# The transpose of the first weight matrix: from TensorE and ScalarE to crossbar transfers issued by SyncE

## The chip, the cores and the metric

The kernel runs on one core of one Trainium2 chip. A core has TensorE (PE, matrix products into PSUM), VectorE (DVE), ScalarE (ACT), GpSimd (POOL) and SyncE (SP, which here only issues transfers), and 16 DMA engines that move data between HBM and SBUF and inside SBUF. Each engine works through its own queue of instructions in order; semaphores hold an instruction until what it needs is there. The metric is device time in microseconds (us) for one execution; times given are medians of several runs.

## The reference

Inputs are x (8 x 4160 x 192), weight_gen (8 x 4160 x 8 heads x 7 taps), and three matrices w1, w2 (192 x 1024) and w_out (1024 x 192), all float32. First a dynamic convolution over time with softmax weights, then a two-layer network that takes the larger of two hidden products:

```python
w = softmax(weight_gen, axis=-1)                     # over the 7 taps
y[b, s, h, :] = sum_k w[b, s, h, k] * x_pad[b, s + k, h, :]
h1, h2 = y @ w1, y @ w2
out = np.maximum(h1, h2) @ w_out
```

x_pad is x with six rows of zeros ahead of each sequence. The output has 33280 rows of 192.

## The kernel before

**The split of the mathematics.** The maximum is written as max(h1, h2) = h1 + relu(h2 - h1). So the kernel computes a hidden product with the difference wd = w2 - w1, a relu on ACT, and a product with w_out (wo); and it adds y @ (w1 @ w_out). The 192 x 192 matrix w1 @ w_out is called w10. It is formed once, on TensorE, in w10_product (line 650): 16 matmuls whose stationary operand is w1t, the transpose of w1 with the 1024 hidden channels on the partitions, in eight blocks of 128 x 192, and whose moving operand is wo. w10_copies (line 662) then moves it from PSUM to the tile w10 (shown in the profile as "w") by three copies on ACT. How w1t comes about is what the change is about.

**Tiling.** The 33280 rows lie as 260 columns of 128 partitions. They go through in batches of 16 columns; a batch is loaded as xb_t (16 columns and a halo of 6 columns that is copied from the batch before, load_halo, line 123) and wg_t (the raw softmax weights). ACT takes exponentials (exp_sum, weights) and logarithms (ln), DVE sums (red) and subtracts (shift). DVE's mul (line 173) multiplies x by the weights for all 7 taps into m_t; adds (line 188) sums the taps into y_t. For the first two batches units of 4 columns are used instead: PE sums the taps and transposes them at once (sum_transpose, line 239) and ACT casts the result to yt. From the third batch on, transpose (line 212) has SP issue a crossbar transfer from y_t to yt, SBUF to SBUF.

**Products.** hid_tile (line 291) multiplies a tile of yt with wd into PSUM (hdp, later hd); relu moves it to rd_t; out_first (line 345) adds y @ w10 and the products of rd_t with wo, out_second the other half of the rows; evac (line 377) copies results to o_t, and SP stores them.

**Order.** The order on each engine is written out by hand (a manual schedule): what is emitted first runs first on its engine. The stretch of the change is the prologue, lines 512 to 693. SP issues the loads of the first weights and of the first x in order, the last being load_wg(1, ...) (line 553). POOL issues two further pieces of x for batch 0, w_out, the first half of x for batch 1 and its halo, in that order. ACT copies w1 in float32 (tiles ws) to bf16 in three pieces, as w1["E"] (rows 0 to 127 of w1, two halves of 512 channels, lines 578 and 633) and w1["T"] (rows 128 to 191, where partitions 0 to 63 hold channels 0 to 511 and partitions 64 to 127 the others, line 632). PE does a matmul on an identity matrix at the start (keep_warm), the first tap sums and the hidden tiles 0 to 3, then w1_transposed (line 594), hidden tiles 4 and 5, a tap sum, hidden tiles 6 and 7, and w10_product. The tile tp of w1_transposed takes a turn in a pool of two PSUM pairs (tag "op") that yps, pw and op_ps share. ACT copies tp to w1t after the relus of tiles 4 and 5 (line 673). behind(first, load) makes a load wait for another instruction.

Of the kernel before, what the change touches and what calls it, by code (L numbers as in the profile page):

```python
# [9 lines left out]
FP32 = mybir.dt.float32  # L10
BF16 = mybir.dt.bfloat16
# [12 lines left out]
def kernel(  # L24
# [9 lines left out]
    nc = tc.nc  # L34

    B, S, D = x.shape
    H, K = weight_gen.shape[2], weight_gen.shape[3]
    F = moe_w1.shape[1]
    P = 128
    PAD = K - 1  # L40
    WGC = H * K
    FCH = F // P
    HF = F // 2
# [20 lines left out]
    for b, (c0, n) in enumerate(BATCHES):  # L64
# [21 lines left out]
    ps = {k: first_ps.enter_context(tc.tile_pool(name="pps_" + k, bufs=2, space=bass.MemoryType.PSUM))  # L86
          for k in ("h", "o")}
# [22 lines left out]
    def load_x(b, o, n, halo=True):  # L110

        if b not in xb_ts:
            xb_ts[b] = pxb.tile([P, (16 + PAD) * D], BF16, name="xb_t", tag="xb")
        load = nc.gpsimd.dma_start(  # L114
            out=xb_ts[b][:, (PAD + o) * D:(PAD + o + n) * D],
            in_=bass.AP(tensor=x.tensor, offset=(BATCHES[b][0] + o) * D,
                        ap=[[CPP * D, P], [1, n * D]]),
        )
        if b > 0 and o == 0 and halo:
            load_halo(b)  # L120
        return load
# [37 lines left out]
    def weights(b, o):  # L159

        w = dict(pieces(b))[o]
        if b not in en_ts:
            en_ts[b] = pen.tile([P, 16 * WGC * 2], BF16, name="en_t", tag="en")
        J = 2 if w == 4 and b < 2 else 1
        N = w * H // J
        for j in range(J):
            nc.scalar.activation(  # L167
                out=_sub(en_ts[b], (o * WGC + j * N * K) * 2, [[2 * N, K], [2, N], [1, 2]]),
                in_=_sub(wg_ts[b], (o * H + j * N) * K, [[1, K], [K, N], [0, 2]]), func=AF.Exp,
            )  # L170


    def mul(b, o):

        n = dict(pieces(b))[o]
        if n == 4 and b < 2:
            m_out = _sub(m_t, K * o * D, [[64, 2], [P, K * 6], [1, 64]])
            x_in = _sub(xb_ts[b], o * D, [[2 * D, 2], [D, K], [1, 2 * D]])
        else:
            m_out = m_t[:, K * o * D:K * (o + n) * D]  # L180
            x_in = _sub(xb_ts[b], o * D, [[D, K], [1, n * D]])
        return nc.vector.tensor_tensor(  # L182
            out=m_out, in0=x_in,
            in1=_sub(en_ts[b], o * WGC * 2, [[2, K * n * H], [0, G // 2], [1, 2]]),
            op=ALU.mult,
        )
# [46 lines left out]
    def half(j):  # L233
        return slice(64 * j, 64 * j + 64)
# [56 lines left out]
    def hid_tile(t):  # L291


        u = TILES[t][0]
        fs, w = chunks(t)
        for f in fs:
            for s in range(3):
                for j in range(2):
                    nc.tensor.matmul(  # L299
                        hid_out(t, f, j), lhsT=wd_at(j, s, f // 4, f % 4 * P, P),  # L300
                        rhs=_sub(yt_ts[u][half(j), :], (s + j) % 3 * P, [[3 * P, w // P], [1, P]]),
                        start=(f == fs[0] and s == 0), stop=(f == fs[-1] and s == 2),
                        skip_group_check=True,
                    )
# [121 lines left out]
    OUTS, c = [[], [], []], 0  # L426
# [8 lines left out]
    def room(g):  # L435

        t0, n = GROUPS[g]
        if "c" in ps:
            ab = ps["ab"].tile([P, 2048], FP32, name="hd2", tag="ab")
            for t in range(t0, t0 + n - 1):  # L440
                hd_at[t] = ab, (t - t0) * 1024
            hd_at[t0 + n - 1] = ps["c"].tile([P, 1024], FP32, name="hd1", tag="c"), 0
        else:
            for t in range(t0, t0 + n):
                hd_at[t] = ps["h"].tile([P, 1024], FP32, name="hdp", tag="hd"), 0
        rd = prd.tile([P, 3 * 1024], BF16, name="rd_t", tag="rd")
        for t in range(t0, t0 + n):
            rd_at[t] = (rd, t - t0)
        return rd
# [56 lines left out]
    ident = consts.tile([P, P], BF16, name="ident")  # L506
# [5 lines left out]
    with tc.tile_pool(name="pstage", bufs=1) as pstage:  # L512
# [7 lines left out]
        for p0, p1 in ((1, 16), (16, P)):  # L520
            nc.sync.dma_start(  # L521
                out=xs[p0:p1, 0:PAD * D],
                in_=bass.AP(tensor=x.tensor, offset=(p0 * CPP - PAD) * D,
                            ap=[[CPP * D, p1 - p0], [1, PAD * D]]),
# [20 lines left out]
        for wi, wsrc in enumerate((moe_w1, moe_w2)):  # L545
            for h in range(2):
                nc.sync.dma_start(
                    out=ws["T", wi][half(h), :],
                    in_=bass.AP(tensor=wsrc.tensor, offset=P * F + h * HF, ap=[[F, 64], [1, HF]]),
# [20 lines left out]
        for o in (0, 4, 8, 12):  # L570
            weights(0, o)
        nc.vector.tensor_copy(out=xb_ts[0][:, PAD * D:(PAD + 4) * D],
                              in_=xs[:, PAD * D:(PAD + 4) * D])
        first_mul = mul(0, 0)
        w1 = {kind: pstage.tile([P, w], BF16, name="w1" + kind)
              for kind, w in (("E", F), ("T", HF))}
# [14 lines left out]

        w1t = pstage.tile([P, FCH * D], BF16, name="w1t")

        def w1_transposed():

            tp = ps["o"].tile([P, 1024], FP32, name="tp", tag="op")[:, :].bitcast(BF16)
            for at, kind, nr in ((0, "E", P), (P, "T", 64)):
                for fi in range(FCH):
                    o = fi // 4 * 1024 + fi % 4 * D
                    rows, c = (slice(0, P), fi) if kind == "E" else (half(fi // 4), fi % 4)  # L600
                    nc.tensor.matmul(
                        tp[:, o + at:o + at + nr],
                        lhsT=w1[kind][rows, c * P:(c + 1) * P],
                        rhs=ident[rows, rows], is_transpose=True, skip_group_check=True,
                    )
            return tp

        warm = ps["h"].tile([P, 1024], FP32, name="warm", tag="hd")

        def keep_warm(times):  # L610
# [11 lines left out]
            out=wo[:, :].rearrange("p (f d) -> p f d", d=D),  # L622
            in_=bass.AP(tensor=moe_w_out.tensor, offset=0, ap=[[D, P], [P * D, FCH], [1, D]]),
# [7 lines left out]

        nc.scalar.copy(out=w1["T"], in_=ws["T", 0])
        nc.scalar.copy(out=w1["E"][:, HF:F], in_=ws["E", 0][:, HF:F])
        rd = room(0)
        hid_tile(0)
        relu(rd, 0, 1)
# [8 lines left out]
        ln(1)  # L645
        shift(1)
        mul(0, 12)
        tp = w1_transposed()

        def w10_product():  # L650

            pw = ps["o"].tile([P, 1024], FP32, name="pw", tag="op")
            for at, c0 in ((0, 0), (512, 64)):
                for fi in range(FCH):
                    nc.tensor.matmul(
                        pw[:, at:at + D], lhsT=w1t[:, fi * D + c0:fi * D + c0 + P],
                        rhs=wo[:, fi * D:(fi + 1) * D],
                        start=(fi == 0), stop=(fi == FCH - 1), skip_group_check=True,
                    )
            return pw  # L660
# [9 lines left out]
        hidden(2)  # L670
        behind(relu_of[5], load_wg(2, nc.gpsimd))
        load_x(1, 8, 8)
        for h in range(2):
            nc.scalar.copy(out=w1t[:, 4 * h * D:4 * (h + 1) * D], in_=tp[:, h * 1024:h * 1024 + 4 * D])
        weights(1, 0)
        mul(1, 0)
        sum_transpose(2)
# [142 lines left out]
```

## Time and profile before

| | us |
|---|---|
| median of 3 runs (lowest to highest) | 411.19 (410.9 to 411.44) |
| profiled execution, from its first to its last instruction | 409.1 |
| PE busy | 398.8 |
| DVE busy | 374.4 |
| ACT busy | 357.4 |
| POOL busy | 68.7 |
| the transposes of w1 on PE (line 601), two groups of 8 | 0.62 and 0.30 |
| the copies tp to w1t on ACT (line 674), 2 | 1.56 |

The profile gives no other time of that execution than its span. It is one execution; "busy" counts neither waits nor the issue of transfers. A share of busy time is a mean over stages with different limits, so what a change in one stretch is worth has to be read there: from the timeline of that stretch, from the waits and from the chain of waits that ended last.

### The profile page before, as it was taken

The page shows a single profiled execution, that of the slowest core. Times are in us where ns is not written, and L with a number is a line of the kernel's source. Part 1 is how long each engine was busy: PE and PEld are TensorE (multiplying, and loading weights), DVE is VectorE, ACT ScalarE, POOL GpSimd, SP SyncE. Part 2 cuts the span into 40 slices and gives each one's busy share as a digit, 9 for nine tenths or more (in the row PEclk, how much of TensorE's full clock was granted, in tenths as well). Part 3 has the DMA queues.
Part 4 walks back from the last instruction along what each step waited for, and adds up shares of the span by engine and source line. Part 5 has one row for each costly group of instructions (what it writes and reads, how often), then busy time and mean ns, then how long its engine had stood idle before and what let it go on. Part 6 is the DMA issues. An engine that isn't in the chain of part 4 may idle for free.

```text
span 409.1 us, 15992 instructions
## 1 busy us (share of the span) xinstructions
PE 398.8 (97%) x7350; PEld 317.1 (78%) x7350; DVE 374.4 (92%) x219; ACT 357.4 (87%) x424; POOL 68.7 (17%) x101
## 2 busy tenths in 40 slices
PE   7999999999999999999999999999999999999995
PEld 2688999677777777777777777777787777787795
DVE  6999999999999999999999999999999999999000
ACT  6899989999999988999988999988999989888771
POOL 0321101222211021221101221210122212210000
PEclk9999999999999999999999999999999999999998
DMA  8966667658657874963796497489648648744513
GB/s 245 250 152 164 116 151 186 143 143 184 150 97 219 217 118 99 260 176 74 224 195 146 96 251 180 82 195 238 120 106 241 166 64 244 151 89 79 213 61 136
DMA packets 60384, 65.68 MB, mean 161 GB/s; under 512 B 47615, under 2 KB 48511, under 8 KB 60318
## 3 DMA queue, kind: packets, MB, share of 16 engines
q1 hardware_dynamic: 51934, 40.54, 36.0%
q0 software_dynamic: 8240, 24.04, 29.5%
q8 instruction: 57, 0.93, 0.9%
q10 hardware_dynamic: 144, 0.10, 0.1%
q14 instruction: 9, 0.07, 0.1%
HBM read 35.96 MB, written 25.56 MB: 150 GB/s over the span
## 4 chain that ended last, share of the span: by engine, by line
DVE 73%; PE 17%; issue 4%; DMA 4%; SPq 0%; DVEq 0%; ACT 0%
DVE m_t L182 37%; DVE m_t L198 15%; DVE m_t L204 10%; PE op_ps L339 9%; PE hd L299 7%; DVE sum_t L147 3%; DVE y_t L207 3%; DVE wg_t L156 3%; DMA xs<-in_x_dram 3%; PE op_ps L351 2%; DMA yt<-y_t 1%; DVE wd L582 0%; DVE xb_t L618 0%; SPq L521 0%; SPq L104 0%
## 5 line engine op out<-in xcount | busy, mean ns | idle before, releaser
L309 ACT ACTIVATE rd_t<-hd 128x1024 bf16<-128x1024 f32 (+1 forms) x206 | 234.6, 1189 | 28.0 <-PE hd L299 26.5
L339 PE MATMUL op_ps<-wo,rd_t 64*128 64x192 bf16 x4160 | 210.6, 243 | 0.1
L339 PEld LDWEIGHTS <-rd_t 64*128 64x128 bf16 x4160 | 180.8, 94 | 15.7 <-ACTq L372 0.3
L299 PE MATMUL hd<-yt,wd 64*128 64x512 bf16 (+1 forms) x1584 | 187.3, 360 | 1.4 <-ACT rd_t L309 1.2
L182 DVE TENSOR_TENSOR m_t<-xb_t,en_t 128x10752 bf16<-128x10752 bf16 (+1 forms) x37 | 187.4, 5071 | 0.2
L299 PEld LDWEIGHTS <-wd 64*128 64x128 bf16 x1776 | 94.1, 94 | 43.3 <-issue 3.3
L224 POOL CAST gate<-yt 128x1 f32<-128x1 bf16 x29 | 34.0, 1171 | 275.7 <-DMA yt<-y_t 275.7
L198 DVE TENSOR_TENSOR m_t<-m_t 128x4608 bf16<-128x4608 bf16 (+1 forms) x32 | 76.8, 2401 | 0.1
L395 ACT COPY o_t<-op_ps 128x384 f32<-128x384 f32 (+1 forms) x99 | 57.3, 591 | 13.4 <-PE op_ps L339 13.3
L351 PE MATMUL op_ps<-w,yt 64*128 64x192 bf16 x780 | 55.5, 243 | 1.1 <-ACT o_t L395 1.0
L351 PEld LDWEIGHTS <-yt 64*128 64x128 bf16 x780 | 38.4, 94 | 17.5 <-issue 2.1
L204 DVE TENSOR_TENSOR m_t<-m_t 128x3072 bf16<-128x3072 bf16 (+1 forms) x29 | 50.0, 1724 | 0.1
L167 ACT ACTIVATE en_t<-wg_t 128x896 bf16<-128x896 f32 (+2 forms) x45 | 35.3, 820 | 0.0
L207 DVE TENSOR_TENSOR y_t<-m_t 128x1536 bf16<-128x1536 bf16 (+1 forms) x29 | 27.3, 941 | 0.5
L385 DVE COPY o_last<-op_ps 128x192 f32<-128x192 f32 x1 | 0.4, 358 | 25.9 <-ACT o_last L385 25.9
L156 DVE TENSOR_TENSOR wg_t<-wg_t,sum_t 128x280 f32<-128x280 f32 (+5 forms) x46 | 22.0, 481 | 0.0
L147 DVE TENSOR_REDUCE sum_t<-e_t 128x64 f32<-128x448 f32 (+2 forms) x31 | 19.6, 636 | 2.6 <-ACT e_t L135 2.6
L114 POOL DMA_DIRECT2D xb_t<-in_x_dram x33 | 17.7, 535 | 23.3 <-ACT rd_t L309 11.8
L135 ACT ACTIVATE e_t<-wg_t 128x896 f32<-128x896 f32 (+2 forms) x18 | 16.1, 899 | 2.5 <-DMA wg_t<-in_weight_gen_dram 2.5
L309 ACT ACTIVATE rd_t<-hdp 128x1024 bf16<-128x1024 f32 x16 | 16.2, 1048 | 0.6 <-PE hdp L299 0.6
L613 PE MATMUL warm<-ident 128*128 128x512 bf16 x38 | 11.0, 457 | 2.6 <-DVE ident L560 2.6
L299 PE MATMUL hdp<-yt,wd 64*128 64x256 bf16 x192 | 12.9, 269 | 0.1
(46 smaller groups left out, 73.6 us busy)
## 6 DMA issues: line engine op xcount, KB each, us to landing
out_dram<-o_t SPq DMA_DIRECT2D x28, 768.0 KB, 5.0
xb_t<-in_x_dram POOLq DMA_DIRECT2D x30, 384.0 KB, 5.2
wg_t<-in_weight_gen_dram POOLq DMA_DIRECT2D x14, 448.0 KB, 5.2
xb_t<-xb_t POOLq DMA_DIRECT2D x16, 288.0 KB, 5.2
out_dram<-o_t SPq DMA_DIRECT2D x8, 384.0 KB, 2.9
wg_t<-in_weight_gen_dram SPq DMA_DIRECT2D x2, 448.0 KB, 4.5
xs<-in_x_dram SPq DMA_DIRECT2D x2, 384.0 KB, 6.0
xb_t<-in_x_dram POOLq DMA_DIRECT2D x3, 192.0 KB, 5.1
```

Source lines behind the costliest of these rows:

```text
L156: nc.vector.tensor_tensor(out=w_t, in0=w_t, in1=_sub(s_ts[b], hs.start, [[1, hs.stop - hs.start], [0, K]]), op=ALU.subtract)
L167: nc.scalar.activation(out=_sub(en_ts[b], (o * WGC + j * N * K) * 2, [[2 * N, K], [2, N], [1, 2]]), in_=_sub(wg_ts[b], (o * H + j * N) * K ...
L182: return nc.vector.tensor_tensor(out=m_out, in0=x_in, in1=_sub(en_ts[b], o * WGC * 2, [[2, K * n * H], [0, G // 2], [1, 2]]), op=ALU.mult,)
L198: nc.vector.tensor_tensor(out=taps(0, 1, 3), in0=taps(0, 1, 3), in1=taps(3, 1, 3), op=ALU.add)
L204: nc.vector.tensor_tensor(out=taps(0, 2, 2), in0=taps(0, 2, 2), in1=taps(1, 5, 2), op=ALU.add)
L207: nc.vector.tensor_tensor(out=_sub(y_ts[b], o * D, [[64, 2], [P, 3 * w // 2], [1, 64]]), in0=taps(0, 1, 1), in1=taps(2, 1, 1), op=ALU.add,)
L224: nc.gpsimd.tensor_copy(out=gate, in_=yt[:, 0:1])
L299: nc.tensor.matmul(hid_out(t, f, j), lhsT=wd_at(j, s, f // 4, f % 4 * P, P), rhs=_sub(yt_ts[u][half(j), :], (s + j) % 3 * P, [[3 * P, w // ...
L309: relu_of[t0] = nc.scalar.activation(out=rd[:, k * 1024:(k + n) * 1024], in_=hd[:, at:at + n * 1024], func=AF.Relu)
L339: return nc.tensor.matmul(op_out(c), lhsT=rd[half(r), k * 1024 + at:k * 1024 + at + P], rhs=wo[half(r), f * D:(f + 1) * D], start=False, s ...
L351: nc.tensor.matmul(op_out(c + j), lhsT=yt_ts[u][half(j), (3 * i + (s + j) % 3) * P:(3 * i + (s + j) % 3 + 1) * P], rhs=w10[half(j), s * D: ...
L395: nc.scalar.copy(out=_sub(o, c % 24 * D, [[D, len(qs)], [h * D, 2], [1, D]]), in_=_sub(tile_, at + (qs[0] - p) * D, [[D, len(qs)], [512, 2 ...
```

## The change

The 16 transposing matmuls and ACT's two copies from PSUM to w1t are taken out. In their place SP issues four crossbar transfers that read the bf16 copies of w1 in SBUF and write w1t in SBUF: one for each half of w1["E"] (128 partitions by 512) and one for each half of w1["T"] (64 partitions by 512). They are emitted directly after ACT's last copy of w1, in the order E first half, T first half, T second half, E second half. SP issued nothing between load_wg(1, ...) and the first output store before. w10_product and all that follows stay as they are.

```diff
         w1t = pstage.tile([P, FCH * D], BF16, name="w1t")
 
-        def w1_transposed():
-
-            tp = ps["o"].tile([P, 1024], FP32, name="tp", tag="op")[:, :].bitcast(BF16)
-            for at, kind, nr in ((0, "E", P), (P, "T", 64)):
-                for fi in range(FCH):
-                    o = fi // 4 * 1024 + fi % 4 * D
-                    rows, c = (slice(0, P), fi) if kind == "E" else (half(fi // 4), fi % 4)
-                    nc.tensor.matmul(
-                        tp[:, o + at:o + at + nr],
-                        lhsT=w1[kind][rows, c * P:(c + 1) * P],
-                        rhs=ident[rows, rows], is_transpose=True, skip_group_check=True,
-                    )
-            return tp
+        def w1_transposed(kind, h):
+
+            out_ = w1t[:, 4 * h * D:4 * (h + 1) * D].rearrange("p (f d) -> p f d", d=D)
+            if kind == "E":
+                nc.sync.dma_start_transpose(out=out_[:, :, 0:P], in_=w1["E"][:, h * HF:(h + 1) * HF])
+            else:
+                nc.sync.dma_start_transpose(out=out_[:, :, P:D], in_=w1["T"][half(h), :])
...
         nc.scalar.copy(out=w1["T"], in_=ws["T", 0])
         nc.scalar.copy(out=w1["E"][:, HF:F], in_=ws["E", 0][:, HF:F])
+        for kind, h in (("E", 0), ("T", 0), ("T", 1), ("E", 1)):
+            w1_transposed(kind, h)
...
         mul(0, 12)
-        tp = w1_transposed()
-
         def w10_product():
...
         load_x(1, 8, 8)
-        for h in range(2):
-            nc.scalar.copy(out=w1t[:, 4 * h * D:4 * (h + 1) * D], in_=tp[:, h * 1024:h * 1024 + 4 * D])
         weights(1, 0)
```

## The prediction

> **What bounds the kernel now.** I read the page first, section 1 for the busy shares:
>
> ```profile
> ## 1 busy us (share of the span) xinstructions
> PE 398.8 (97%) x7350; PEld 317.1 (78%) x7350; DVE 374.4 (92%) x219; ACT 357.4 (87%) x424; POOL 68.7 (17%) x101
> ```
>
> TensorE (PE) and VectorE (DVE) are both nearly full, so a saving on one of them counts only where the other does not hold it back. The chain of waits, in order of time (start, length, what), says who does, around the change and late in the kernel:
>
> ```profile
> 12.90 0.57 DVE xb_t L618
> ...
> 25.73 5.82 DVE m_t L182 x2
> ...
> 328.23 5.23 DMA yt<-y_t
> 333.50 0.82 PE hd L299 x6
> ```
>
> From 12.90 to 328 us the chain lies on DVE. The trace has only 0.76 us of idle DVE time between 12.7 and 328.3 us. At 328.23 a crossbar transfer carries the last such y_t to yt, PE picks it up at 333.50, and from there PE sets the end. The list of waits says how tight that meeting is (us in total, times, longest):
>
> ```profile
> PE hd L299 <- DMA yt<-y_t: 0.2, 1, 0.2
> ```
>
> PE waits for a crossbar transfer once in the whole kernel, 0.2 us, at 333.3. I set each unit's landing beside PE's first hidden-layer matmul on it: the margin is 7.3 us for the first transfer (issue 56.23), 2.6 us near 215 us and 0.04 us at 333.45. PE idles 3.8 us in all after 2.0 us, so it runs almost without a break and slowly catches up with DVE. Hence two paths end together. A DVE delay early on comes out at the end whole, less about 0.04 us; a PE delay comes out less what later waits absorb; a PE or ACT gain comes out only until PE meets DVE, some 0.2 us.
>
> Next the timeline of the stretch that is changed (start, length, engine, line):
>
> ```profile
> 19.41 0.62 PE L601 MATMUL tp<-ident,w1E 128*128 128x128 bf16 x8
> 19.96 0.30 PE L601 MATMUL tp<-ident,w1T 64*128 64x64 bf16 x8
> ...
> 22.00 1.02 PE L248 MATMUL yps<-ident,m_t 64*128 64x64 bf16 x57
> ...
> 22.98 1.56 ACT L674 COPY w1t<-tp 128x768 bf16<-128x768 bf16 x2
> ...
> 25.12 1.49 PE L655 MATMUL pw<-wo,w1t 128*128 128x192 bf16 x16
> ```
>
> **Part one, what goes away.** PE loses 16 transposes, 0.62 + 0.30 = 0.92 us. They lie between hidden tiles 3 and 4. Tile 4 needs the PSUM buffer that ACT's relu of tile 2 empties (19.16 plus about 1.02 = 20.18), and its first matmul starts at 20.26 already; tile 5 waits for the next relu, about 21.15. Then sum_transpose(2) starts at 22.00, as DVE finishes mul(0, 8) (19.00 + 2.95 = 21.95). So the 0.92 us turn into waits for ACT and DVE, and nothing moves at 22.00: 0 us. ACT loses two copies, 2 x 0.866, 1.56 us on the clock with their overlap. What follows in ACT's queue is weights(1, 0), then the cast of yps, which needs PE's sum_transpose(2) (23.32 + 0.56 = 23.88), relu 6, and w10_copies, which need PE's w10_product (25.12 + 1.49 = 26.61; the first copy starts at 26.65). PE reaches w10_product through sum_transpose(2) and hidden tiles 6 and 7 (23.71 + 1.48 = 25.19), none of which waited for the copies. So ACT idles before 26.65 and continues as before: 0 us. DVE's mul(1, 0) had its weights at 24.35 + 0.80 = 25.15 and starts at 25.73 because DVE is full; earlier weights bring nothing. Half of a PSUM pair comes free sooner (tp no longer has a turn), but pw and the next yps take buffers that were empty before too. If all of this cover failed, the most it could bring is 0.92 us of PE, since ACT's 1.56 us run beside it.
>
> **Part two, what is added: issue.** Four crossbar transfers on SP's queue, behind load_wg(1, ...) at 10.03; the next SP instruction is the first output store at 32.41, so SP is free in between and nobody stands behind them. The first waits for ACT's copy of w1E (10.01 + 0.60 = 10.61), the second and third for w1T (14.78 + 0.62 = 15.40), the fourth for the other half of w1E (15.30 + 0.62 = 15.92). The nearest rows are those of the yt transfers, in the list of DMA issues (median us from issue to landing) and in the rows on yt (ns for which SP is held: least, median, most):
>
> ```profile
> yt<-y_t SPq DMA_TRANSPOSE x29, 3.9
> ```
>
> ```profile
> L216 SPq DMA_TRANSPOSE yt<-y_t x29: 1316/1435/2807, 56.2 to 379.2; - x29
> ```
>
> With a hold of 1.4 us each, SP starts the second at 15.4, the third at 16.8, the fourth at 18.2. A whole yt (12 blocks, 1536 packets of 256 bytes) lands in 3.6 to 5.4 us; the fourth is a third of that, so 18.2 + 5.4 = 23.6 is late for it. PE needs the first half of w1t at 25.12 and the second half four matmuls later, about 25.5. Margin 1.9 us: 0 us on PE. With the longest hold each time (2.81) the fourth starts at 21.0 and lands by 26.4 at worst, 0.9 us too late. I take the median, as the chunks are smaller than a yt.
>
> The Trainium skill speaks against the change here: "VectorE: DVE Perf Modes", section "The three transpose paths", puts a 128x128 bf16 transpose at 390 ns on TensorE and 1309 ns through the DMA crossbar, and its rules take TensorE where PSUM will do as destination. By an estimate from that page, the twelve blocks' worth one after another would last 12 x 1.309 = 15.7 us from 15.4, and PE would stall about 6 us (near 417 us); the rows above, 12 blocks in 3.9 us, don't agree with such a sum.
>
> **Part three, what is added: traffic.** The four move 8 blocks of 128x128 and 8 of 64x128, again 1536 packets of 256 bytes if a half block costs half. Alone, a yt's packets pass in 2.0 us on all 16 engines; where PE's instruction fetch falls among them they take 3.0 to 3.5, and by the time that packets were held the dearest came to 4.1. The windows (length, PE, PEld, DVE, ACT, POOL, clock, DMA share, GB/s) show what they meet:
>
> ```profile
> 16.00:18.00 2.00, 1.83 (x96) 1.47 (x92) 1.92 (x6) 2.00 (x3) 0.00 (x0) 1.00 1.28 156
> 18.00:20.00 2.00, 1.99 (x34) 1.45 (x32) 2.00 (x2) 2.00 (x3) 0.54 (x1) 1.00 1.29 207
> 20.00:22.00 2.00, 1.92 (x33) 1.34 (x33) 2.00 (x2) 2.00 (x4) 0.00 (x0) 1.00 0.69 197
> 22.00:24.00 2.00, 1.70 (x91) 1.57 (x92) 2.00 (x2) 2.00 (x4) 0.56 (x2) 1.00 0.05 18
> ```
>
> The DMA engines are full with POOL's loads until about 21 us and then almost idle until POOL's next load (issue 23.44). The first transfer stands behind wg_t's load in SP's queue (landing 15.3) and meets xb_t columns 8 to 15: these land at 17.0 and 17.8, needed at 19.00 and 22.86, so 0.7 to 1.4 us there are covered. wo lands at 20.8, needed at 25.12: covered. Tight is mul(1, 0) at 25.73: its columns land at 22.6 and its halo (xb_t<-xb_t, issue 18.41) at 23.6, 2.1 us ahead. Delay between 0 (the transfers use gaps) and 4.1 us (dearest row, all of it added to the slowest engine); I take 2.0, the uncontended row, because those engines are idle after 22: landing 25.6, still 0.1 us early. Sum: 0 us.
>
> **Part four, phases.** PE has 32 fewer instructions (16 matmuls, 16 weight loads), at some 35 such instructions a us 0.9 us of its stream, so its instruction fetches shift against the yt transfers. One fetch at 331.3 to 332.2 stretched the transfer behind the 0.2 us wait; it may now miss it, or hit another whose margin is near 1 us. Worth -0.2 to +0.4 us; I take 0. Total: span 409.1 + 0 + 0 + 0. The median of the runs, 411.2, lies 2.1 us above the span (the profile gives no other time of that execution), and I carry that over: 411.2 us.
>
> **The rivals.** *Slower: the halo comes late.* The place is mul(1, 0) on DVE at 25.73; behind it in DVE's queue stand all later products, with 0.76 us of idle time in 316 us to make it up. It decides from a delay of 2.1 us on; a loss over 0.8 us needs 3.0. At 4.1 us the stall is 2.0 us: about 413.2 us. For it: no row shows a crossbar transfer beside sustained POOL loads, and a single 16 KB fetch on one engine already costs one 1.0 to 1.5 us. Against: idle engines from 22 us.
> *Slower: w1t comes late.* If each of the four waits until the one before has landed (the yt transfers are 6 to 12 us apart and can't show it), then at a yt's 3.9 us the last lands at 15.4 + 3 x 3.9 = 27.1, 1.6 us after 25.5. Behind w10_product stand w10_copies and weights(1, 4) on ACT (28.38, for DVE's mul(1, 4) at 28.60), so DVE stalls 1.4 us: 412.6 us. Against: the pieces are a third and a sixth of a yt.
> *Faster: the 0.92 us of PE come through*, if relu and DVE do not hold 20.2 and 22.0, and the fetch leaves 333 us: 411.2 - 0.92 = 410.3. Against: the margin of 0.04 us at 333.45 and DVE's full queue.
>
> **The numbers.** Measurement can tell about 0.2% (0.8 us) from no change. Covered everywhere 0.67, with small stalls under 0.8 us in it; halo late by more 0.14; w1t late by more 0.13; faster 0.06. Prediction 411.2; the range goes from 410.6 (runs spread 0.3 below the median, and the phases) to 413.0, which takes in most of both slow cases. Faster 0.06, within 0.2% 0.67, slower 0.27.
>
> **What would show it.** Right: no L601 and no w1t<-tp rows; four transfers landing before 25.1; PE's L655 at 25.1; DVE's products at 22.86 and 25.73 without idle time before them; ACT idle 0.7 us or so before L664; PE's wait for yt still near 333 us. Wrong: idle DVE time before L182 put down to xb_t<-xb_t or xb_t<-in_x_dram (halo), or PE waiting at L655 for w1t with the following DVE product late (w1t), or sum_transpose(2) before 22.0 (faster).

## The result, and the profile after

The changed kernel took 414.10 us (median of 10 runs, 413.55 to 416.27), the kernel before 411.27 beside it on the same chip (10 runs, 410.65 to 413.95): a ratio of 1.0066 with a 95% interval from 1.0044 to 1.0088. It is slower by 2.8 us, and lies 1.1 us above the upper end of the predicted range.

The profiled execution took 414.07 us with a span of 412.3 us, 3.2 us more than the span of before. Section 1 of its page, and from section 4 the shares of the chain that ended last:

```profile
PE 398.4 (97%) x7334; PEld 317.0 (77%) x7334; DVE 374.7 (91%) x219; ACT 356.4 (86%) x422; POOL 69.0 (17%) x101
...
PE 83%; ACT 10%; DMA 3%; issue 2%; DVE 0%; SPq 0%; DVEq 0%; ACTq 0%
```

PE lost its 32 instructions and ACT its two copies, and no engine became busier in a way that would explain 3.2 us. What grew is waiting. The chain now runs over PE to the end, where before it lay on DVE for 73% of the span; its stretch in the prologue says where the time went (start, length, what):

```profile
21.29 0.83 PE hdp L299 x12
22.13 1.20 PE yps L248 x73
23.33 2.47 issue
25.80 0.35 PE yps L248 x11
26.15 2.56 PE hdp L299 x24
28.71 1.79 PE pw L649 x16
30.52 0.48 ACT w L658
```

In the middle of sum_transpose(2) PE stands for 2.47 us, and the releaser is "issue": no semaphore, no other engine, no transfer of data. The 73 matmuls before and the 11 after belong to the same loop over the same tile. Before, a stop of 0.30 us stood in the same sum (23.02 to 23.32). In the timeline of the kernel before, with the wait before a group in brackets:

```profile
23.32 0.56 PE L248 MATMUL yps<-ident,m_t 64*128 64x64 bf16 x27 [0.30 <-issue]
23.71 1.48 PE L299 MATMUL hdp<-yt,wd 64*128 64x256 bf16 x24
```

The timeline of the changed kernel shows SP's issues, then PE, DVE and ACT:

```profile
10.92 1.32 SPq L598 DMA_TRANSPOSE w1t<-w1E  x1
15.54 2.46 SPq L600 DMA_TRANSPOSE w1t<-w1T  x2
18.10 1.23 SPq L598 DMA_TRANSPOSE w1t<-w1E  x1
...
25.80 0.35 PE L248 MATMUL yps<-ident,m_t 64*128 64x64 bf16 x11 [2.47 <-issue]
25.96 2.75 PE L299 MATMUL hdp<-yt,wd 64*128 64x256 bf16 x24
28.64 1.84 PE L649 MATMUL pw<-wo,w1t 128*128 128x192 bf16 x16
...
26.79 2.96 DVE L182 TENSOR_TENSOR m_t<-xb_t,en_t 128x5376 bf16<-128x5376 bf16 x1 [0.90 <-DMA xb_t<-xb_t]
32.28 2.96 DVE L182 TENSOR_TENSOR m_t<-xb_t,en_t 128x5376 bf16<-128x5376 bf16 x1 [2.53 <-ACT en_t L167]
...
30.52 0.48 ACT L658 CAST w<-pw 128x384 bf16<-128x384 f32 x1 [2.03 <-PE pw L649]
```

After the stop the hidden tiles 6 and 7 (line 299) last 2.75 us instead of 1.48, and w10_product 1.84 instead of 1.49. The windows say why (length, PE, PEld, DVE, ACT, POOL, clock, DMA share, GB/s):

```profile
22.00:24.00 2.00, 1.33 (x76) 1.14 (x74) 2.00 (x3) 1.86 (x4) 0.44 (x1) 1.00 2.05 61
24.00:26.00 2.00, 0.20 (x13) 0.20 (x14) 1.89 (x1) 0.00 (x0) 0.64 (x2) 1.00 0.44 131
26.00:28.00 2.00, 2.00 (x30) 1.58 (x23) 1.21 (x1) 1.34 (x2) 0.00 (x0) 0.50 1.09 326
28.00:30.00 2.00, 2.00 (x21) 1.50 (x17) 1.75 (x1) 0.49 (x1) 0.00 (x0) 0.65 0.54 108
```

PE does nearly nothing from 24 to 26, and after that its granted clock is 0.50; the records put the half clock at 25.99 to 29.40. So the path to the first copy of w10 on ACT lost 2.17 us (stop, 2.47 - 0.30), 1.27 us (tiles 6 and 7) and 0.35 us (w10_product), 3.79 together; that copy starts at 30.52 instead of 26.65, 3.87 late. weights(1, 4) stands behind w10_copies in ACT's queue, and DVE's mul(1, 4) waits 2.53 us for it, starting at 32.28 instead of 28.60. From there nothing is made up for 200 us: PE reaches the first yt that a crossbar transfer brings (unit 8) at 72.80 instead of 68.93, again 3.87 late, and unit 16 is as late. Near units 27 to 31 0.66 us comes back (PE's wait for yt at 333 us is gone) and 0.25 us is lost again behind them; the span is 3.2 us longer.

**What stands at the stop.** The trace records show that PE's instruction stream is read in packets of 16 KB on the queue called "instruction", 57 in the kernel. Counted over PE's records (matmuls, weight loads and a few others), PE stops at record 705 in both kernels, and the stops of the other kernels below lie at 449, 705, 961 and 1217: 256 apart. The packet that ends shortly before PE goes on took 0.975 us before (21.01 to 21.99) and 2.925 us after (21.45 to 24.37). PE goes on 1.33 and 1.43 us after its end. The DMA view of 20 to 25 us has that packet among these:

```profile
q1 hardware_dynamic: 1063, 0.25, 100.5%
q0 software_dynamic: 109, 0.25, 41.6%
q8 instruction: 1, 0.02, 3.7%
```

Columns are packets, MB, and the time of the packets as a share of 16 engines. q1 are the crossbar packets; before, this queue had none there, and two instruction packets together had 2.9%. By the records no 256-byte packet ended from 16 to 19 us, while POOL's loads kept the engines; then 28, 68 and 613 of them did in the three us from 19 to 22, and 64, 210 and 22 from 22 to 25. The rows on w1t have SP's hold in ns (least, median, most) and then the time to landing:

```profile
L598 SPq DMA_TRANSPOSE w1t<-w1E x2: 1231/1274/1316, 10.9 to 18.1; - x2
L600 SPq DMA_TRANSPOSE w1t<-w1T x2: 1172/1206/1239, 15.5 to 16.8; - x2
...
DMA to landing us min/median/max: 5.0/8.4/8.7
```

SP went on as quickly as predicted, but three of the four took 8.1 to 8.7 us and landed at 23.61, 25.48 and 26.82.

### The profile page after: what moved, and what is told of

Its sections match the earlier page's. It is cut to its first block, busy times and chain, and to the rows that moved or that the text cites. A ratio compares the mean times of both kernels' runs of the same rounds, so it can differ in the third digit from the quotient of the medians.

```text
span 412.3 us, 15968 instructions
## 1 busy us (share of the span) xinstructions
PE 398.4 (97%) x7334; PEld 317.0 (77%) x7334; DVE 374.7 (91%) x219; ACT 356.4 (86%) x422; POOL 69.0 (17%) x101
## 4 chain that ended last, share of the span: by engine, by line
PE 83%; ACT 10%; DMA 3%; issue 2%; DVE 0%; SPq 0%; DVEq 0%; ACTq 0%
PE op_ps L339 38%; PE hd L299 36%; PE op_ps L351 7%; ACT rd_t L309 6%; DMA ws1T<-in_moe_w_dram 2%; PE hdp L299 1%; ACT en_t L167 1%; DMA wg_t<-in_weight_gen_dram 1%; ACT o_t L395 1%; ACT yt L255 1%; ACT e_t L135 1%; PE pw L649 0%; PE yps L248 0%; ACT sum_t L151 0%; DVE xb_t L612 0%
## 5 line engine op out<-in xcount | busy, mean ns | idle before, releaser
L339 PEld LDWEIGHTS <-rd_t 64*128 64x128 bf16 x4160 | 180.7, 94 | 15.7 <-ACTq L372 0.3
L299 PE MATMUL hdp<-yt,wd 64*128 64x256 bf16 x192 | 14.1, 287 | 1.0 <-ACT rd_t L309 0.8
L248 PE MATMUL yps<-ident,m_t 64*128 64x64 bf16 x564 | 9.8, 190 | 3.6 <-issue 2.5
```

Of the source, the lines that this page charges most:

```text
L299: nc.tensor.matmul(hid_out(t, f, j), lhsT=wd_at(j, s, f // 4, f % 4 * P, P), rhs=_sub(yt_ts[u][half(j), :], (s + j) % 3 * P, [[3 * P, w // ...
L339: return nc.tensor.matmul(op_out(c), lhsT=rd[half(r), k * 1024 + at:k * 1024 + at + P], rhs=wo[half(r), f * D:(f + 1) * D], start=False, s ...
```

## The experiments

Theory F (starved): the crossbar transfers of the second to fourth piece delay PE's instruction read at record 705; PE stops, its clock is halved, and w10_copies hold weights(1, 4) and with it DVE. Rival W: PE or the order of things waits for w1t itself. Rival H: the halo of batch 1 comes late to DVE. Rival R: taking the transposes off PE does harm. A last question was whether the stop alone is enough, and where the border of the block lies.

The table has every kernel that was run. "unit 8" is the start of the first hidden matmul on unit 8 in the profiled execution, against 68.93 of before, and "span" that execution's span against 409.1. The two columns lie within 0.75 us of each other in all rows but that of halo_behind (1.2): what the first 70 us lose comes out at the end.

| kernel | median us (runs) | ratio, 95% interval | stop at record 705, us | unit 8 | span |
|---|---|---|---|---|---|
| after | 414.10 (10) | 1.0066, 1.0044 to 1.0088 | 2.47 | +3.87 | +3.2 |
| remove_only | 411.87 (10) | 0.9992, 0.9968 to 1.0016 | none | +0.53 | +0.9 |
| add_only | 415.52 (5) | 1.0085, 1.0055 to 1.0114 | 3.01 | +5.31 | +4.6 |
| add_first | 411.03 (11) | 0.9982, 0.9965 to 0.9998 | none | +1.99 | +2.5 |
| add_rest | 414.82 (4) | 1.0081, 1.0058 to 1.0105 | 1.81 | +4.70 | +4.0 |
| shift_before | 414.66 (4) | 1.0078, 1.0052 to 1.0104 | 2.49 | +3.83 | +3.4 |
| shift_after | 416.77 (4) | 1.0131, 1.0092 to 1.0171 | 1.41 | +5.68 | +5.8 |
| stall_only | 414.67 (7) | 1.0070, 1.0049 to 1.0091 | 1.00 | +4.10 | +3.7 |
| halo_late | 414.22 (4) | 1.0067, 1.0041 to 1.0092 | none | +3.05 | +3.2 |
| halo_behind | 412.07 (10) | 1.0008, 0.9983 to 1.0033 | none | +1.23 | +2.4 |
| early_three | 413.10 (12) | 1.0033, 1.0001 to 1.0064 | 0.77 | +2.51 | +2.1 |

The profiled execution of add_first was its slowest (413.35, against 410.41 to 411.41 of the others), and that of halo_behind lay 1.3 us over its median; both had a late start of the whole prologue, so their last two columns are too high by about as much. In the profiled executions of remove_only, stall_only, add_rest and early_three the prologue began 0.4 to 1.0 us late as well.

### The removal alone: remove_only

```diff
+        nc.gpsimd.memset(w1t, 0.0)               # behind load_x(1, 0, 8)
...
-        for kind, h in (("E", 0), ("T", 0), ("T", 1), ("E", 1)):
-            w1_transposed(kind, h)
```

> The kernel after without its four crossbar transfers: w1t is filled with zeros by one POOL memset (so w1 @ w_out is left out of the result), and TensorE's transposes and ACT's two copies stay away. Theory F (the loss comes from the crossbar packets holding up PE's instruction read, which starves PE at its record 705, and from the half clock that follows): 411.2 us, no half clock, PE's gap at record 705 back to 0.3 to 0.5 us. Theory W (PE or ACT waits for a late w1t): also 411.2. Theory R (taking PE's 0.92 us away opens a pause near 19.6 to 20.4 us that costs the clock): about 412.5 to 414, with a half clock near 26 us. My part one (the removal is worth nothing): within 0.5 us of 411.2.

It is as fast as before within what these runs can tell. The waits in its timeline are those that part one of the prediction named, PE for the relu where the transposes had been:

```profile
21.33 1.75 PE L299 MATMUL hdp<-yt,wd 64*128 64x256 bf16 x24 [0.79 <-ACT rd_t L309]
...
25.63 1.49 PE L648 MATMUL pw<-wo,w1t 128*128 128x192 bf16 x16
```

w10_product keeps its 1.49 us, no stop of PE is put down to "issue" here, and ACT idles 0.74 us before w10_copies. So R falls: it asked for 412.5 us or more, a ratio of 1.0026 at least. The interval alone would still hold a gain of 0.92 us (0.9978); that PE's 0.92 us were worth nothing is read from the timelines, where PE waits for the relu in their place and sum_transpose(2) starts no earlier (22.08 in the changed kernel, 22.00 before).

### The addition alone: add_only, add_first, add_rest

All three keep the transposes on PE and send crossbar transfers into a tile that nobody reads; add_only all four, add_first the first, add_rest the other three.

```diff
+        w1x = pstage.tile([P, FCH * D], BF16, name="w1x")
+        def w1_crossed(kind, h):
+            out_ = w1x[:, 4 * h * D:4 * (h + 1) * D].rearrange("p (f d) -> p f d", d=D)
+            if kind == "E":
+                nc.sync.dma_start_transpose(out=out_[:, :, 0:P], in_=w1["E"][:, h * HF:(h + 1) * HF])
+            else:
+                nc.sync.dma_start_transpose(out=out_[:, :, P:D], in_=w1["T"][half(h), :])
...
+        for kind, h in (("E", 0), ("T", 0), ("T", 1), ("E", 1)):   # add_first, add_rest: a part
+            w1_crossed(kind, h)
```

> The kernel before, with the same four crossbar transfers at the same place, into a tile that nobody reads; w1t still comes from TensorE and ACT. Theory F: the traffic alone makes the loss: PE gap of about 2.5 us near 23 us at record 705, half clock for some 3 us behind it, 413.5 to 414.5 us. Theory W: nobody waits for the new tile, so 411.2 us. Theory H (only the late halo counts): DVE idle 0.9 us before mul(1, 0), no more: 411.5 to 412.1 us.

> The kernel before plus only the first of the four crossbar transfers (w1E's first half, issued near 11 us), into a tile that nobody reads. It lands near 15.9 us, just as POOL's loads begin. Theory F (the packets that stand among POOL's loads until 21 to 25 us hold up the instruction read): 411.2 us, PE's gap at record 705 no longer than 0.5 us. If any crossbar transfer costs, by its packets: a third of the loss, about 412.3 to 412.8 us.

> The kernel before plus the last three crossbar transfers only (issued from 15.5 us on), into a tile that nobody reads. Theory F: they stand among POOL's loads, land after 23 us, the instruction read that begins near 21.5 us takes 2 to 3 us in place of 1, PE stops 2 to 3 us at record 705: 413.5 to 415.5 us, all of add_only's loss. If the loss goes by the number of packets: two thirds, about 413.9 us with a short gap.

add_only has the whole loss and 1.0 us more than theory F was expected to give, though no instruction waits for its tile, so W is not needed for it. Its PE and DVE lines in the timeline:

```profile
26.33 0.56 PE L248 MATMUL yps<-ident,m_t 64*128 64x64 bf16 x27 [3.01 <-issue]
...
28.43 2.96 DVE L182 TENSOR_TENSOR m_t<-xb_t,en_t 128x5376 bf16<-128x5376 bf16 x1 [2.31 <-DMA xb_t<-xb_t]
33.04 2.96 DVE L182 TENSOR_TENSOR m_t<-xb_t,en_t 128x5376 bf16<-128x5376 bf16 x1 [1.66 <-ACT en_t L167]
```

The stop falls before the same 27 matmuls as in the kernel before, at 3.01 us instead of 0.30, and its instruction packet took 2.466 us. add_first has no loss (the packet took 0.976 us, no stop put down to "issue"), add_rest all of it:

```profile
25.20 0.56 PE L248 MATMUL yps<-ident,m_t 64*128 64x64 bf16 x27 [1.81 <-issue]
31.37 0.52 PE L248 MATMUL yps<-ident,m_t 64*128 64x64 bf16 x23 [1.86 <-issue]
```

Here the packet took 2.264 us, and a second stop stands one block on, at record 961. Its transfers landed at 26.0, 26.3 and 26.7. So the harm sits in the three pieces that are issued at 15.5 us and later, into POOL's loads; the one that is issued before them costs nothing.

### The border of the block: shift_before and shift_after

Both replace six of the matmuls that warm PE up at the start by 86 small ones, which puts 160 more records ahead of everything that follows; shift_before does so in the kernel before, without any crossbar transfer, shift_after in the changed one.

```diff
-        keep_warm(30)
+        keep_warm(24)
+        for i in range(86):
+            nc.tensor.matmul(warm[:, i % 2 * 512:i % 2 * 512 + 64], lhsT=ident[half(i % 2), :],
+                             rhs=ident[half(i % 2), 0:64], start=True, stop=True, skip_group_check=True)
```

> The kernel after with 80 more instructions pairs on PE in the warm-up (6 matmuls of 512 columns give way to 86 small ones), so that everything behind them stands 160 PE records later and the borders of PE's 256-record instruction reads fall elsewhere: at what were records 545 and 801, not 705. Theory F: the gap inside sum_transpose(2) goes; any gap moves to the new borders (near 21.3 and 26.5 us) and is shorter; what is left is the wait for w1t (its last landing was 26.8 against 25.5 needed) and the late halo: 412.0 to 413.3 us. Theory W or H: the gap's place is not tied to the record, the time stays near 414.0.

> The kernel before with the same 160 extra PE records in the warm-up, as the control for shift_after (416.8 us). If the shift by itself is harmless: 411.2 us, and then shift_after's loss of 5.3 us is all due to the crossbar transfers. If new borders of the instruction reads hurt by themselves (gaps at records 705 and 961 in other code, and later in the kernel): 412 to 414 us, and the transfers cost the difference.

shift_before is 3.3 us slower than before by the medians (414.66 against 411.39), 0.7 us above the range expected for borders that hurt by themselves, with no crossbar transfer near. In its timeline the stop has moved with the record, out of the tap sum into hidden tile 4, and DVE waits as in the changed kernel:

```profile
23.21 2.71 PE L299 MATMUL hdp<-yt,wd 64*128 64x256 bf16 x23 [2.49 <-issue]
...
29.01 2.96 DVE L182 TENSOR_TENSOR m_t<-xb_t,en_t 128x5376 bf16<-128x5376 bf16 x1 [3.06 <-ACT en_t L167]
```

The read itself was quick, 0.936 us. But it began at 20.99 us, as before (21.01), although PE stood at record 705 already at 20.72 and in the kernel before only at 23.02. So its start is not set by how far PE has come: over all kernels here PE stood between record 470 (halo_late, at 20.32 us) and 705 when it began. What does set it is open. That POOL's loads hold it up would fit before, where they thin out at 21 us; in early_three, below, it began at 22.20 while they kept the DMA engines full until 24.0. What PE can do without harm in this prologue is to need the block later than 21.0 + 0.95 + 1.33 = 23.3 us: before it came 0.30 us early.

In shift_after, which I expected to be no slower than the changed kernel, the time is the longest of all (416.77). Its stops lie in hidden tile 5 and, at record 961, inside w10_product:

```profile
23.42 0.59 PE L299 MATMUL hdp<-yt,wd 64*128 64x256 bf16 x7 [1.41 <-issue]
28.80 0.41 PE L652 MATMUL pw<-wo,w1t 128*128 128x192 bf16 x3 [0.93 <-issue]
```

Its read began at 20.94 and took 0.922 us, ahead of the bulk of the crossbar packets; w10_copies start at 29.24, earlier than in the changed kernel, and yet it lost more afterwards, in waits of PE at 41.6 (1.64 us), 51.6 (0.81) and 58.9 (0.54). My expectation was a miss. Counted over PE's records these three waits stand at records 1729, 2241 and 2497, which are borders of blocks too, and PE goes on 1.59, 1.40 and 1.25 us after the end of a read (41.68, 50.97 and 58.14 us). The five stops make 5.33 us of the 5.68 by which unit 8 is late. These later reads were quick (0.90 to 0.95 us); why they began no earlier is open.

### The stop alone: stall_only

No crossbar transfer; PE is made to wait, between the tap sum and hidden tile 6, for a small tile that DVE writes late.

```diff
+        late = pstage.tile([P, 64], BF16, name="late")
+        nc.vector.memset(late, 0.0)              # on DVE, ahead of mul(1, 0)
...
+        pw = ps["o"].tile([P, 1024], FP32, name="pw", tag="op")
+        nc.tensor.matmul(pw[:, 0:64], lhsT=ident, rhs=late, start=True, stop=True, skip_group_check=True)
```

> The kernel before without any crossbar transfer of w1, and with one small matmul on PE behind sum_transpose(2) that waits for a small DVE memset emitted after mul(0, 12), so that PE stands still from about 23.9 to 25.8 us as it did in the kernel after (DVE loses 0.1 us to the memset). Theory F: the pause of PE by itself, and the half clock if it follows, make most of the loss: 412.8 to 414.5 us; 412.5 if the clock stays whole. If the loss came from DMA (H) or from w1t (W): 411.2 to 411.6, as PE would catch up.

```profile
24.88 0.56 PE L248 MATMUL yps<-ident,m_t 64*128 64x64 bf16 x27 [1.00 <-issue]
26.86 0.19 PE L680 MATMUL pw<-late,ident 128*128 128x64 bf16 x1 [1.42 <-DVE late L676]
...
31.69 2.96 DVE L182 TENSOR_TENSOR m_t<-xb_t,en_t 128x5376 bf16<-128x5376 bf16 x1 [2.13 <-ACT en_t L167]
```

PE stood for 2.42 us in two parts, its clock stayed whole, and DVE waited 2.13 us for en_t; the loss is that of the changed kernel (414.67), 2.2 us more than I had expected with a whole clock. It shows that a halt of PE in this place is paid through ACT's queue and DVE, without any crossbar traffic. It is not a clean copy: its prologue was some 0.7 us late, and the stop at 705 of 1.00 us came on top of the one that I built in.

### The halo alone: halo_late and halo_behind

```diff
-        load_x(1, 0, 8)
+        load_x(1, 0, 8, halo=False)
+        idle = pstage.tile([P, FCH * D], BF16, name="idle")
+        for _ in range(7):
+            nc.gpsimd.memset(idle, 0.0)
+        load_halo(1)                             # halo_late
```

```diff
+        return nc.gpsimd.dma_start(...)          # load_halo
-        load_x(1, 0, 8)
+        load_x(1, 0, 8, halo=False)
-        behind(relu_of[5], load_wg(2, nc.gpsimd))
+        behind(relu_of[5], load_halo(1))         # halo_behind
+        load_wg(2, nc.gpsimd)
```

> The kernel before, without crossbar transfers of w1; seven POOL memsets of a scratch tile stand between load_x(1, 0, 8) and load_halo(1), so that the halo of batch 1 is issued near 24.4 us in place of 18.4 and lands near 27. DVE then idles 1 to 2 us before mul(1, 0), PE is not touched directly. If a DVE delay comes out whole at the end, as the prediction said: 412.1 to 413.2 us. If DVE's slack to PE hides it: 411.2 us, and the late halo was no part of the loss.

> The kernel before without crossbar transfers of w1; the halo copy of batch 1 is issued by POOL only behind the relu of tile 5 (near 23.2 us in place of 18.4), with no memsets beside DVE as in halo_late. It lands near 26 to 27 us, DVE idles 0.3 to 1.3 us before mul(1, 0). PE and the instruction read are not touched. If a DVE delay comes out whole, less 0.04 us: 411.5 to 412.5 us, that is the DVE idle time added to 411.2. If PE's lag hides it: 411.2.

halo_late was spoiled by its own means: beside POOL's memsets DVE's copy of wd took 1.54 us, where it takes 0.28 in the kernel before, and PE waited for it.

```profile
19.18 1.54 DVE L589 COPY wd<-wd 64x512 bf16<-64x512 bf16 x1
...
29.54 5.83 DVE L182 TENSOR_TENSOR m_t<-xb_t,en_t 128x5376 bf16<-128x5376 bf16 x2 [0.97 <-DMA xb_t<-xb_t]
```

It still tells how an early delay comes out: mul(1, 0) starts 3.81 us late and the span is 3.2 us longer. halo_behind has the wait and no stop of PE, though its prologue began 1 us late:

```profile
28.34 5.83 DVE L182 TENSOR_TENSOR m_t<-xb_t,en_t 128x5376 bf16<-128x5376 bf16 x2 [1.33 <-DMA xb_t<-xb_t]
```

A halo late by 1.33 us costs 0.8 us by the medians (412.07 against 411.25), with an interval that holds zero. In the changed kernel the wait was 0.90 us, and mul(1, 4) could not have started before 32.24 in any case, since en_t was not done earlier (31.55 + 0.69). So H happened, and by these rows adds nothing to the 3.2 us there.

### Issuing earlier: early_three

The first three transfers are issued at 11.35 to 13.98 us, the two of w1["T"] some 2.8 us earlier than in the changed kernel, and the fourth piece stays on PE and ACT.

```diff
+        nc.scalar.copy(out=w1["T"], in_=ws["T", 0])          # moved up, behind the first half of w1["E"]
+        for kind, h in (("E", 0), ("T", 0), ("T", 1)):
+            w1_crossed(kind, h)
...
+        tp = w1_transposed()                                 # four transposes, w1["E"] second half
...
+        nc.scalar.copy(out=_sub(w1t, 4 * D, [[D, 4], [1, P]]), in_=_sub(tp, 0, [[P, 4], [1, P]]))
```

> A version between the two: ACT casts the T part of w1 right behind the first half of the E part (near 11 us, where ACT stood idle), so that three of the four crossbar transfers are issued by about 14 us and stand directly behind wg_t's load in SP's queue; the second half of E is transposed by TensorE (4 matmuls) and copied by ACT (one copy). Theory F: as add_first showed, packets that pass before POOL's loads cost nothing; if the three land by 18 us, 410.8 to 411.5 us and PE's gap at record 705 at most 0.5 us. If T's two stay among POOL's loads until 21 us or later: 412.5 to 414.5 us with a gap of 1 to 2 us. Nothing here can gain more than the 0.2 us that PE waits for yt near 333 us.

The runs spread from 410.65 to 415.87; the median is 413.10.

```profile
24.41 0.39 PE L248 MATMUL yps<-ident,m_t 64*128 64x64 bf16 x15 [0.77 <-issue]
...
30.16 0.34 PE L248 MATMUL yps<-ident,m_t 64*128 64x64 bf16 x11 [1.45 <-issue]
```

The read for record 705 took 0.974 us again, and its stop is 0.77 us; but the transfers of w1["T"] landed only at 20.27 and 21.48, still caught among POOL's loads, and a stop of 1.45 us stands at record 961. By the medians it lies between the kernel before and the changed one; its interval (1.0001 to 1.0064) overlaps with that of the changed kernel (1.0044 to 1.0088). With a removal that is worth nothing, no placement of the transfers could be better than the kernel before.

## Why the prediction was wrong

**Part one held.** The removal was priced at 0, with the covers named. remove_only measures 0.9992 (0.9968 to 1.0016), and its waits are the ones named.

**Part two failed in the landing.** SP's holds were 1.17 to 1.32 us, below the 1.4 that I took, and the fourth transfer was issued at 18.10 (predicted 18.2). But I took the landing from a whole yt at 3.6 to 5.4 us, and those rows come from transfers that the kernel keeps apart from POOL's loads: behind each of the 29, a small POOL instruction (gate, line 224) waits for the landing before POOL issues its next loads. The list of waits of the kernel before has it (us in total, times, longest), and while the packets of those transfers moved, POOL's took at most 4% of the 16 engines' time:

```profile
POOL gate L224 <- DMA yt<-y_t: 275.7, 29, 13.8
```

The four new transfers have no such guard. Here the three later pieces, each smaller than a yt, took 8.1 to 8.7 us. The fourth landed at 26.82, later than the worst case I had worked out (26.4). In the end this cost nothing by itself: PE came to w10_product at 28.64, after the landing. Without the stop it would have waited, so the w1t rival was hidden, not refuted: in shift_after, where PE came there at 26.48, a weight load did wait 0.19 us for w1t. add_only shows that the rival is not needed for the loss.

**Part three is the step that failed and decided.** I had priced the traffic by what it meets, and listed xb_t, wo and the halo; the sum of 0 us has no term for PE's instruction read. The halo came 3.1 us late (26.67 instead of 23.57), between the 2.0 I took and the 4.1 I kept as the bound, and DVE waited 0.90 us. What was not on the list is the instruction read of PE, although two things in the trace of before spoke of it: the stop of 0.30 us with no releaser in PE's waits at 23.0, which means that PE was already early for that block, and the two packets on the instruction queue. I had even used such reads, but only as what slows a yt transfer down. The other direction, that crossbar packets slow the read, I did not ask. The size follows from rows: the read ended 2.38 us later (24.37 against 21.99), and as its cover was below zero, the stop grew by nearly all of it, 2.17 us. Part four has the same hole: it moved the reads by 32 instructions and priced them only against the transfers at 333 us.

**The half clock** was not in the sum. The granted clock fell to 0.50 for 3.41 us after a stop of 2.47 us, worth 1.27 + 0.35 us in the profiled execution. The Trainium skill, "TensorE: Matmul & The Clock Gate", section "Why this matters for your kernels", asks for no idle gaps of PE over about 3 us; here less was enough. Stops of 2.47 (after), 2.49 (shift_before) and 3.01 us (add_only) came with half clock, in shift_before from 0.76 us before the stop's end on; 2.38 (add_first, 10.78 to 13.16 us), 1.81 and 1.86 (add_rest) and 1.00 and 1.42 (stall_only) did not. How much of the loss is due to it stays open: add_rest and stall_only lose as much without it, and within add_rest the runs with a mean clock of 0.994 and 0.995 took 414.73 and 415.00 us, those with 1.000 took 414.91 and 414.47.

**The path to the end** was read rightly in the main. "A DVE delay early on comes out at the end whole, less about 0.04 us; a PE delay comes out less what later waits absorb": 3.87 us at units 8 and 16 came out as 3.2. The 0.04 us held only for one transfer: the one issued at 328.23 before, with an instruction read among its packets, took 5.23 us, and in the changed kernel (331.91), with none among them, 3.95. So DVE's delay of 3.69 us did not come out whole, and PE, 3.22 us late there, set the end. The queue behind w10_product that the w1t rival named (w10_copies, weights(1, 4), mul(1, 4)) is the one that carried the loss; only the reason why w10_product was late was another.

**The rule that spoke against the change** gave PE stalled for w1t near 417 us. The verdict of that rule (take TensorE) agrees with the result, its price does not explain it: the four pieces issued at 10.92 to 18.10 had all landed by 26.82, where the sum of 15.7 us from 15.4 gives 31.1, and the loss came from what their packets did to another reader.

**On the reads**, the skill's "Runtime: NRT & Kernel Launch", section "Instruction fetch mechanics", has blocks of 16 KiB and 256 instructions on a DMA queue of their own, and the cost of crossing a border mostly hidden. The trace agrees with the first (borders 256 records apart, 57 packets with 0.93 MB) and, in this prologue, not with the second: 0.30 us before, 1.81 to 3.01 us with the three late transfers where the border lies in the tap sum, and 2.49 us without any when PE needs the block earlier.

**What stays open.** That the three late pieces lengthen the read is shown by adding and leaving them out: it took 2.3 to 2.9 us in after, add_only and add_rest, and 0.89 to 0.98 in the other nine (shift_after has the pieces too, but its read began ahead of most of their packets). How they do it is not shown, and neither is why they hardly move while POOL's loads run. It is not their number alone: add_rest's read met 84 of the 256-byte packets, after's 526. Nor does either kind of traffic alone do as much: beside POOL's loads, which filled the DMA engines, early_three's read took 0.97 us, and later in the kernel before reads that met some 500 packets of a yt without POOL's loads took at most 1.66. No run kept POOL's loads apart from the new transfers, as the gate does for yt.

## What to carry to other kernels

Before adding transfers to a full stretch, list everything that reads through the DMA engines there, the engines' own instructions included: an idle time of PE with "issue" as its releaser, standing at a border of 256 of its instructions, marks a read that has no slack, and what delays that read comes through nearly whole (here 2.17 of 2.38 us). Time that is freed on an engine counts only if the work behind it can start earlier; look for that first, since it sets the most a change can bring. And take the duration of a transfer from a row with the same neighbours, not from the same kind of transfer in a quiet stretch; where the kernel itself keeps two kinds of traffic apart, as the gate does, ask what a new transfer beside both will meet.

## What was not expected of the hardware

- PE stops at the borders of its instruction blocks: moving its code by 160 records, and nothing else of weight, cost 3.3 us of 411 (shift_before, 1.0078, 1.0052 to 1.0104).
- A crossbar transfer of a third of a yt took 8.7 us from issue to landing beside POOL's loads, a whole yt 3.7 us (median) in the same execution.
- Beside memsets on POOL a copy of 64 x 512 bf16 on DVE took 1.54 us instead of 0.28 (halo_late).
